# The first guess of 1/Q in MoE1's block 0: kept in the PSUM bank of h

## The chip, the cores and the metric

The kernel runs on one core of a Trainium2 chip. The metric is device time in microseconds (us) of one execution. Before the change the median of three runs is 865.55 us (864.24 to 868.3).

## The reference

Attention with two kinds of mask (local for heads 0 to 3, strided for 4 to 7) gives x, 2304 tokens by 512. A first MoE layer (MoE1) follows, which is a dense layer with a rational activation, and then a second (MoE2) that sends each token to the expert of its largest logit. Cut to what the change touches:

```python
def _moe_ref(x, w_in, w_out, a, b):        # x 2304x512, w_in 512x2048, w_out 2048x512
    h = x @ w_in
    h2 = h * h
    h3 = h2 * h
    P = a[0] + a[1] * h + a[2] * h2 + a[3] * h3
    Q = 1.0 + np.abs(b[0]) * np.abs(h) + np.abs(b[1]) * h2
    g = P / (Q + 1e-06)
    return (g @ w_out).astype(np.float32)
```

## The kernel before

MoE1 is cut into 6 blocks of 384 tokens, and each block into 16 slices of 128 hidden columns: 96 steps s, where block 0 is s = 0 to 15. Attention is cut into units U of one half of one pair of heads. While block 0 runs, units 8 to 15 still pass through, and the weights of MoE1 are still being split into high and low parts. All this is interleaved by hand, and each engine works off its own instructions in the order in which they are written.

One step passes through these named operations (the names are those of the order tables):

- `m1` (PE, line 516): 12 matmuls into a PSUM bank h. There are two such banks.
- `fA` (ACT, 446 and 447): A = |h| and G = a3 h + a2 in SBUF.
- `fP` (POOL, 451 and 452): Q = (b1 A + b0) A in SBUF, without the 1 of the reference.
- `fD`, `fE` (DVE, 457 and 462): G times h, then (G + a1) times h. `fE` is the last reader of h.
- `rA` (ACT, 470 and 472): Ln of Q + 1 + 1e-6, and Exp of its negative, which gives the first guess y of 1/Q. Either y takes the place of A in SBUF, or it goes into a PSUM bank m (steps 16 to 29, and 64 on).
- `rD`, `rN`, `rG` (DVE): one Newton step and the product with P. With y in A these are lines 481, 488 and 496, and both tensors of each come from SBUF. With y in PSUM they are 479, 486 and 493, and one of the two comes from PSUM.
- `sA` (ACT, 383) and `sP` (line 506, POOL or DVE): G into its high part gh and its low part gl. Then `m2` (PE, 527): 9 matmuls into three accumulators.

A unit of attention goes: `qk` (transposes of q and k on PE, copied out by DVE), `sc` (scores, 317), `mx` (row maxima, 340), `ex` (353), `rc` (363 and 365), `nm` (370, on POOL in this stretch), `aT` (transposes on PE, 379), `ae` (copy by ACT), `pv` (408), `xA` (ACT) and `xD` (DVE, 432). A weight is split by `c0A` (ACT, 223), `c0P` (POOL, 229), `c1` and `c1b` (DVE, 233 and 238), `c2A` (ACT or DVE, a cast on line 383) and `c2P` (249).

A window w covers the steps 2w and 2w+1. Its order is a table: `rD@-1` means "run rD up to step 2w-1 now, if what it needs has been written", and the letter after a point names the engine (A for ACT, D for DVE, G for POOL; with several letters they alternate). Windows 0 to 7, called "first", cover block 0. "plain" covers 8 to 14, "attention" 15 to 31, "last" 32 on. `ready` holds the conditions, among them free banks. A, Q and G have two buffers each, so `fA` of a step waits for `sP` two steps earlier.

Of the kernel before, what the change touches and what calls it, by code (L numbers as in the profile page):

```python
# [7 lines left out]
F32 = mybir.dt.float32  # L8
# [4 lines left out]
ACTF = mybir.ActivationFunctionType  # L13
ALU = mybir.AluOpType
# [5 lines left out]
def tile_attention_moe_moe2(  # L20
# [20 lines left out]
    BLK = 384  # L41
# [394 lines left out]
    hid = {}  # L436
# [193 lines left out]
    def keep_warm(n):  # L630
# [38 lines left out]
    def parse(text):
# [24 lines left out]
    done = {}  # L694
# [14 lines left out]
    def ready(T, j):  # L709
        for p, d in need[T]:  # L710
            if done[p] < j + 1 + d and not (j < 9 and (T, p) in (("mx", "aT"), ("ae", "pv"))):
                return False
        if T == "m1":
            i, f = divmod(j, NF)
            if i == 0 and done["c2P"] <= conv_q.index(("i", f)):
                return False
            if not all(log["h"][-1:]):
                return False
            if done["xD"] < (8, 16, 16, 24, 32, 32)[i]:
                return False  # L720
# [136 lines left out]
    def window(w, sch):  # L857
        if w == 8:
            load_w(len(conv_q) - n_load[0])
            for T, eng in (("c2A", "A"), ("c2P", "G"), ("c1b", ""), ("c1", ""), ("c0A", ""), ("c0P", "G")) * 4:  # L860
                run_to(T, len(conv_q), eng)
        if w == 32:
            for _ in range(3):
                run_to("rE", done["rT"], "A")
                run_to("rL", done["rT"], "")
                run_to("rP", done["rT"], "A")
                run_to("rQ", done["rT"], "")
        if w in (8, 15, 32):
# [506 lines left out]
```

## Time and profile before

| | |
|---|---|
| median of three runs | 865.55 us |
| the profiled execution: its own time, its span | 864.46 us, 862.7 us |
| mean granted TensorE clock, as a share of full speed | 0.970 |
| PE busy | 793.3 us, 92% |
| DVE busy | 688.3 us, 80% |
| ACT busy | 536.6 us, 62% |
| POOL busy | 464.1 us, 54% |

The span runs from the first to the last instruction. The engines' shares are means over stages: MoE1's block 0 lies at about 74 to 205 us, its other blocks up to about 620 us, MoE2 behind them. A wait that is told here is the idle time of an engine before an instruction, with what ended it.

### The profile page before, as it was taken

What the parts mean: (1) busy time and instruction counts of PE and PEld (TensorE: products, weight loads), DVE (VectorE), ACT (ScalarE), POOL (GpSimd) and SP (SyncE); (2) the same over time, 40 slices, a digit from 0 to 9 for tenths busy, and PEclk for the clock granted to TensorE, in tenths of its full rate; (3) what the DMA queues carried; (4) which work ended last, traced back from release to release, by engine and by line L of the source; (5) the groups of instructions that cost most, each with busy time, mean ns of one, the idle gap of its engine ahead of it and who ended that gap; (6) DMA issues with size and microseconds to landing.
All of it is one profiled execution on the core that took longest, in us unless ns stands there. A gap on an engine that the chain in (4) does not pass through costs nothing.

```text
span 862.7 us, 15597 instructions
## 1 busy us (share of the span) xinstructions
PE 793.3 (92%) x5301; PEld 678.0 (79%) x5301; DVE 688.3 (80%) x1656; ACT 536.6 (62%) x1397; POOL 464.1 (54%) x463
## 2 busy tenths in 40 slices
PE   6787687788999999999999999999899999999995
PEld 3555576677898787888878888888779999988884
DVE  4999989979777988789888889779865776777772
ACT  3786767565657787888776656666623554555552
POOL 3787878787554444443445668567423444444431
PEclk9989989889999999999999999999999999999998
DMA  8991322200201310122100100302115866776630
GB/s 198 307 263 49 104 84 68 57 8 12 63 1 28 82 45 12 42 61 69 44 9 8 38 2 2 134 1 100 62 27 185 319 220 229 226 240 226 225 117 5
DMA packets 71609, 85.59 MB, mean 99 GB/s; under 512 B 38111, under 2 KB 48607, under 8 KB 71520
## 3 DMA queue, kind: packets, MB, share of 16 engines
q1 hardware_dynamic: 68112, 74.36, 28.1%
q0 software_dynamic: 3120, 10.13, 3.6%
q8 instruction: 44, 0.72, 0.4%
q14 instruction: 45, 0.37, 0.1%
q10 hardware_dynamic: 288, 0.00, 0.0%
HBM read 74.89 MB, written 9.85 MB: 98 GB/s over the span
## 4 chain that ended last, share of the span: by engine, by line
PE 55%; DVE 19%; ACT 11%; POOL 7%; issue 4%; DMA 2%; SPq 0%; another core or an unknown queue 0%; POOLq 0%; DVEq 0%; ACTq 0%
PE h L516 13%; PE o L527 12%; PE h L1166 12%; PE o L1180 11%; ACT S L353 4%; DVE G L496 3%; DVE Q L488 2%; POOL Q L452 2%; DVE Q L481 2%; POOL Q L451 2%; ACT A L470 2%; POOL S L370 1%; ACT A L472 1%; PE m L379 1%; PE zb L632 1%
## 5 line engine op out<-in xcount | busy, mean ns | idle before, releaser
L516 PE MATMUL h<-xh,wi 128*128 128x384 f32 x768 | 219.2, 350 | 1.3 <-DVE G L462 1.3
L527 PE MATMUL o<-wo,gh 128*128 128x512 f32 x576 | 188.8, 409 | 2.1 <-POOL wo L249 1.8
L451 POOL TENSOR_SCALAR Q<-A,coef 128x384 f32<-128x384 f32 x96 | 80.3, 837 | 188.1 <-ACT A L446 187.8
L516 PEld LDWEIGHTS h<-xh,wi 128*128 128x128 f32 x768 | 145.2, 195 | 4.3 <-DVE G L462 2.0
L516 PE MATMUL h<-xl,wi 128*128 128x384 f32 x384 | 132.5, 345 | 4.7 <-DVE xl L432 4.7
L527 PEld LDWEIGHTS o<-wo,gh 128*128 128x128 f32 x576 | 105.8, 191 | 26.6 <-POOL wo L249 2.1
L527 PE MATMUL o<-wo,gl 128*128 128x512 f32 x288 | 116.3, 404 | 0.9 <-POOL gl L506 0.5
L452 POOL TENSOR_TENSOR Q<-Q,A 128x384 f32<-128x384 f32 x96 | 103.5, 1079 | 8.0
L1170 ACT ACTIVATE hh<-h 128x256 fp32r<-128x256 f32 x76 | 29.2, 384 | 98.5 <-PE h L1166 98.5
L1166 PE MATMUL h<-xh,w1h 128*128 128x256 f32 x320 | 89.5, 280 | 0.0
L1166 PE MATMUL h<-xh,w1l 128*128 128x256 f32 x320 | 89.0, 278 | 0.0
L1166 PE MATMUL h<-xl,w1h 128*128 128x256 f32 x320 | 88.9, 278 | 0.0
L470 ACT ACTIVATE A<-Q,coef 128x384 f32<-128x384 f32 x96 | 59.2, 616 | 45.2 <-POOL Q L452 45.0
L353 ACT ACTIVATE S<-S,nb 72x72 f32<-72x72 f32 (+1 forms) x224 | 80.6, 363 | 7.2 <-DVE nb L340 7.2
L516 PEld LDWEIGHTS h<-xl,wi 128*128 128x128 f32 x384 | 74.9, 195 | 6.6 <-DVE xl L432 5.0
L506 POOL TENSOR_TENSOR gl<-G,gh 128x384 fp32r<-128x384 f32 x71 | 74.7, 1052 | 9.6 <-ACT gh L383 9.4
L383 ACT CAST gh<-G 128x384 fp32r<-128x384 f32 x96 | 49.4, 514 | 42.0 <-DVE G L493 25.3
L446 ACT ACTIVATE A<-h 128x384 f32<-128x384 f32 x96 | 46.5, 485 | 40.6 <-PE h L516 40.4
L527 PEld LDWEIGHTS o<-wo,gl 128*128 128x128 f32 x288 | 55.0, 191 | 15.9 <-POOL gl L506 1.8
L457 DVE TENSOR_TENSOR G<-G,h 128x384 f32<-128x384 f32 x96 | 52.3, 545 | 17.1 <-ACT G L447 17.1
L447 ACT ACTIVATE G<-h,coef 128x384 f32<-128x384 f32 x96 | 63.9, 665 | 0.1
L1171 DVE SCALAR_TENSOR_TENSOR hl<-h,hh 128x256 fp32r<-128x256 f32 x76 | 32.2, 424 | 39.7 <-ACT hh L1170 39.7
(212 smaller groups left out, 1908.2 us busy)
## 6 DMA issues: line engine op xcount, KB each, us to landing
w1r<-in_moe_w_dram SPq DMA_DIRECT2D x36, 512.0 KB
w2r<-in_moe_w_dram SPq DMA_DIRECT2D x36, 512.0 KB
rawi<-in_moe_w_in_dram SPq DMA_DIRECT2D x16, 512.0 KB
rawo<-in_moe_w_out_dram SPq DMA_DIRECT2D x16, 512.0 KB
xs<-x SPq DMA_DIRECT2D x18, 256.0 KB
vt<-in_v_dram SPq DMA_DIRECT2D x48, 64.0 KB
rawq<-in_q_dram SPq DMA_DIRECT2D x16, 144.0 KB
rawk<-in_k_dram SPq DMA_DIRECT2D x16, 144.0 KB
```

The lines of the kernel that those rows point to most:

```text
L353: ACT.activation(out=Sv[:, j, c], in_=Sv[:, j, c], func=ACTF.Exp, scale=-1.0, bias=nb[0:nq, u : u + 1], **({"accum_out": rb[0:nq, u : u + ...
L383: (ACT.copy if eng is ACT else eng.tensor_copy)(out, in_)
L447: ACT.activation(out=G, in_=h, func=ACTF.Identity, scale=coef[:, 3:4], bias=coef[:, 2:3])
L451: eng.tensor_scalar(out=Q, in0=A, scalar1=coef[:, 5:6], scalar2=coef[:, 4:5], op0=ALU.mult, op1=ALU.add)
L452: eng.tensor_tensor(out=Q, in0=Q, in1=A, op=ALU.mult)
L457: DVE.tensor_tensor(out=G, in0=G, in1=h, op=ALU.mult)
L470: ACT.activation(out=A, in_=Q, func=ACTF.Ln, bias=coef[:, 6:7])
L506: eng.tensor_tensor(out=gl, in0=G, in1=gh.bitcast(F32), op=ALU.subtract)
L516: PE.matmul(h[:, 0:BLK], lhsT=w[:, o + 128 * kk : o + 128 * kk + 128], rhs=x[:, kk, c0 : c0 + BLK], start=n == 0, stop=n == 11)
L527: PE.matmul(acc[t], lhsT=a[:, ts], rhs=w[:, o : o + 512], start=f == 0 and n == 0, stop=f == NF - 1 and n == 2)
L1166: PE.matmul(h, lhsT=w[kk][:, 128 * f : 128 * f + 128], rhs=x[:, kk, c0 : c0 + TILE], start=n == 0, stop=n == 11)
L1180: PE.matmul(acc, lhsT=a[:, hs], rhs=w[f // 2][:, ws], start=f == 0 and n == 0, stop=f == NH - 1 and n == 2)
```

## The change

- For steps 0 to 14, `rA` writes y over h, in the same PSUM bank. The bank is free for `m1` two steps later only when `rG` has read y, where it was free after `fE` before. Step 15 uses a bank m like steps 16 to 29.
- `rD`, `rN` and `rG` of steps 0 to 15 take the forms with one tensor in PSUM.
- 1 + 1e-6 is written into the instructions (the bias of Ln, and a scalar of DVE), where it was read from a column of coef; the memset of that column goes.
- The order tables are new. In windows 1 to 7 the two steps of a window go side by side (`fD fD fE fE`, `rD rD rN rN rG rG`) rather than one after the other; `sP` of steps 0 to 14 is on DVE and no longer on POOL, and six of the seven casts `c2A` that DVE did are on ACT. On PE the two `m2` come ahead of the second `m1`, which now waits for `rG`, and `m2` runs one step later than before. In "plain" `sP` is all on POOL; in "attention" `pv` comes ahead of `sc`.

```diff
     def ew_p2(s):
         A, Q, G = st[s]
-        h = hid.pop(s)
+        h = hid[s] if y_home(s) == "h" else hid.pop(s)
         DVE.scalar_tensor_tensor(out=G, in0=G, scalar=coef[:, 1:2], in1=h, op0=ALU.add, op1=ALU.mult)
 
-    def y_in_psum(s):
-
-        return 16 <= s < 30 or s >= 64
+    def y_home(s):
+
+        return "h" if s < 15 else "m" if s < 30 or s >= 64 else "A"
 
     def ew_recip(s):
         A, Q, G = st[s]
-        ACT.activation(out=A, in_=Q, func=ACTF.Ln, bias=coef[:, 6:7])
-        y = misc("y")[:, 0:BLK] if y_in_psum(s) else A
+        ACT.activation(out=A, in_=Q, func=ACTF.Ln, bias=1.0 + 1e-6)
+        y = misc("y")[:, 0:BLK] if y_home(s) == "m" else hid.pop(s) if y_home(s) == "h" else A
...
     def ew_2(s):
         y, Q, G = st[s]
-        if y_in_psum(s):
-            DVE.scalar_tensor_tensor(out=y, in0=Q, scalar=coef[:, 6:7], in1=y, op0=ALU.add, op1=ALU.mult)
+        if y_home(s) != "A":
+            DVE.scalar_tensor_tensor(out=y, in0=Q, scalar=1.0 + 1e-6, in1=y, op0=ALU.add, op1=ALU.mult)
...
         "first": """
-        c1@-1 aT@-1 lw@-3 m1@0 c2P.D@-3 c1b@-1 ae.A@-1 fD@-1 pv@-1 c2A.AD@-3 sc@0 rA@-1 lq@0 fE@-1 fA@0
+        aT@-1 m1@0 c2P.D@-3 fD@-1 c1@-2 lq@0 c2A.AD@-3 ae.A@-1 pv@-1 fA@0 rD@0 lw@-3 c1b@-2 fP.G@0 c2A.A@-2 sc@0
...
             if not all(log["h"][-1:]):
                 return False
+            if j >= 2 and y_home(j - 2) == "h" and done["rG"] < j - 1:
+                return False
...
         elif T == "rD":
-            return not y_in_psum(j) or done["fE"] > j
-        elif T in ("pv", "rL", "rQ") or (T == "rA" and y_in_psum(j)):
+            return done["fE"] > j or y_home(j) == "A"
+        elif T in ("pv", "rL", "rQ") or (T == "rA" and y_home(j) == "m"):
             return can_alloc(1)
+        elif T == "rA":
+            return done["fE"] > j or y_home(j) == "A"
```

DVE at the end of window 5 and the start of window 6, before (the second step of the window from its `fE` on; S, rb and xl belong to attention, rawi and rawo are weights being split):

```order
L462 SCALAR_TENSOR_TENSOR G<-G,coef,h 128x384
L481 SCALAR_TENSOR_TENSOR Q<-Q,coef,A 128x384
L488 SCALAR_TENSOR_TENSOR Q<-Q,A 128x384
L496 SCALAR_TENSOR_TENSOR G<-G,coef,Q 128x384
L363 TENSOR_SCALAR rb<-rb 72x8
L365 RECIPROCAL rb<-rb 72x8
L432 TENSOR_TENSOR xl<-m,xh 128x288
L233 SCALAR_TENSOR_TENSOR rawi<-rawi 128x512
L233 SCALAR_TENSOR_TENSOR rawo<-rawo 128x512
L238 SCALAR_TENSOR_TENSOR rawi<-rawi 128x512
```

The same place after (line numbers are one lower there):

```order
L478 SCALAR_TENSOR_TENSOR G<-G,coef,h 128x384 x2
L485 SCALAR_TENSOR_TENSOR h<-Q,h 128x384 x2
L492 SCALAR_TENSOR_TENSOR G<-h,G 128x384 x2
L362 TENSOR_SCALAR rb<-rb 72x8
L364 RECIPROCAL rb<-rb 72x8
L431 TENSOR_TENSOR xl<-m,xh 128x288
L506 TENSOR_TENSOR gl<-G,gh 128x384 x2
L232 SCALAR_TENSOR_TENSOR rawi<-rawi 128x512
L232 SCALAR_TENSOR_TENSOR rawo<-rawo 128x512
L237 SCALAR_TENSOR_TENSOR rawi<-rawi 128x512
```

Both steps now pass through the three operations together, with h where A was, and two `sP` stand between `xD` and the splitting of the weights.

POOL in window 2, before:

```order
L229 TENSOR_SCALAR rawi<-rawi 128x512
L451 TENSOR_SCALAR Q<-A,coef 128x384
L452 TENSOR_TENSOR Q<-Q,A 128x384
L506 TENSOR_TENSOR gl<-G,gh 128x384
L229 TENSOR_SCALAR rawo<-rawo 128x512
L249 TENSOR_TENSOR wi<-rawi,wi 128x512
L249 TENSOR_TENSOR wo<-rawo,wo 128x512
L370 TENSOR_TENSOR S<-S,rb 72x576
L451 TENSOR_SCALAR Q<-A,coef 128x384
L452 TENSOR_TENSOR Q<-Q,A 128x384
L506 TENSOR_TENSOR gl<-G,gh 128x384
```

And after:

```order
L450 TENSOR_SCALAR Q<-A,coef 128x384
L451 TENSOR_TENSOR Q<-Q,A 128x384
L450 TENSOR_SCALAR Q<-A,coef 128x384
L451 TENSOR_TENSOR Q<-Q,A 128x384
L228 TENSOR_SCALAR rawi<-rawi 128x512
L228 TENSOR_SCALAR rawo<-rawo 128x512
L248 TENSOR_TENSOR wi<-rawi,wi 128x512
L248 TENSOR_TENSOR wo<-rawo,wo 128x512
L369 TENSOR_TENSOR S<-S,rb 72x576
```

Both `fP` have moved to the front, the two `sP` have gone, and `nm` (S<-S,rb) is the last of the window.

## Rows read from the trace of the kernel before

**Rows 1.** By stretch: length, busy PE, PEld, DVE, ACT, POOL, granted clock, DMA share, GB/s.

```profile
92.00:205.00 113.00, 91.45 (x569) 77.96 (x567) 101.96 (x220) 68.90 (x196) 90.98 (x77) 0.87 0.18 52
205.00:330.00 125.00, 121.49 (x793) 104.73 (x794) 101.73 (x249) 88.91 (x227) 58.37 (x61) 1.00 0.15 40
```

**Rows 2.** What PE waited for, 74 to 205 us: us in total, times, longest.

```profile
PE m L379 <- POOL S L370: 12.9, 5, 4.4
PE m L290 <- issue: 8.8, 3, 4.0
```

**Rows 3.** DVE by line and shape, 74 to 205 us: busy us, mean ns | idle before.

```profile
L496 DVE SCALAR_TENSOR_TENSOR G<-G,coef,Q 128x384 f32<-128x384 f32 x15 | 17.1, 1137 | 0.5
L488 DVE SCALAR_TENSOR_TENSOR Q<-Q,A 128x384 f32<-128x384 f32 x15 | 16.0, 1068 | 0.5
L481 DVE SCALAR_TENSOR_TENSOR Q<-Q,coef,A 128x384 f32<-128x384 f32 x15 | 13.6, 905 | 8.1 <-ACT A L472 7.0 <-POOL gl L506 1.0
...
L383 DVE COPY kT<-m 128x288 f32<-128x288 f32 x6 | 3.0, 536 | 0.1
...
L383 DVE CAST wi<-rawi 128x512 fp32r<-128x512 f32 x6 | 4.2, 694 | 0.0
```

**Rows 4.** DVE in window 2: start, us, instruction.

```profile
116.50 1.55 DVE L488 SCALAR_TENSOR_TENSOR Q<-Q,A 128x384 f32<-128x384 f32 x1
```

**Rows 5.** POOL in window 2.

```profile
116.14 1.49 POOL L249 TENSOR_TENSOR wi<-rawi,wi 128x512 fp32r<-128x512 f32 x1
...
120.11 1.15 POOL L370 TENSOR_TENSOR S<-S,rb 72x576 f32<-72x576 f32 x1 [0.90 <-ACT G L447]
```

**Rows 6.** DVE's forms with PSUM, whole span, by line.

```profile
L486 DVE SCALAR_TENSOR_TENSOR m<-Q,coef,m 128x384 f32<-128x384 f32 x46 | 28.3, 616 | 0.0
L479 DVE SCALAR_TENSOR_TENSOR G<-G,coef,m 128x384 f32<-128x384 f32 x46 | 28.1, 610 | 19.0 <-ACT m L472 19.0
L493 DVE SCALAR_TENSOR_TENSOR G<-m,G 128x384 f32<-128x384 f32 x46 | 25.6, 557 | 1.6
```

**Rows 7.** Line 506 on DVE: duration ns min/median/max, first and last start.

```profile
L506 DVE TENSOR_TENSOR gl<-G,gh x25: 549/567/1218, 210.8 to 619.9; 128x384 fp32r<-128x384 f32 x25
```

**Rows 8.** DVE at the end of window 1.

```profile
103.26 0.20 DVE L365 RECIPROCAL rb<-rb 72x8 f32<-72x8 f32 x1
...
103.70 0.68 DVE L233 SCALAR_TENSOR_TENSOR rawi<-rawi 128x512 uint32<-128x512 uint32 x1
```

**Rows 9.** POOL beside it.

```profile
103.63 3.57 POOL L370 TENSOR_TENSOR S<-S,rb 72x576 f32<-72x576 f32 x1 [0.90 <-DVE rb L365]
```

**Rows 10.** The chain that ended last: start, us, engine, tile, line.

```profile
107.25 0.69 PE m L379 x8
107.94 3.69 PE h L516 x12
...
158.99 2.34 PE h L516 x12
```

**Rows 11.** ACT by line and shape, 74 to 205 us.

```profile
L353 ACT ACTIVATE S<-S,nb 72x72 f32<-72x72 f32 x32 | 10.9, 341 | 0.0
L447 ACT ACTIVATE G<-h,coef 128x384 f32<-128x384 f32 x16 | 10.6, 661 | 0.0
L470 ACT ACTIVATE A<-Q,coef 128x384 f32<-128x384 f32 x15 | 9.3, 617 | 9.5 <-POOL Q L452 9.5
L472 ACT ACTIVATE A<-A 128x384 f32<-128x384 f32 x15 | 7.9, 525 | 0.5
...
L446 ACT ACTIVATE A<-h 128x384 f32<-128x384 f32 x16 | 7.6, 477 | 7.2 <-PE h L516 7.2
```

**Rows 12.** PE at the start of windows 1, 7 and 8.

```profile
90.58 0.82 PE L379 MATMUL m<-ident,S 96*128 96x96 f32 x6 [0.47 <-POOL S L370]
...
188.32 0.69 PE L379 MATMUL m<-ident,S 72*72 72x72 f32 x8 [1.30 <-POOL S L370]
...
201.99 0.52 PE L516 MATMUL h<-xh,wi 128*128 128x384 f32 x1
```

More of the change, by code (lines that the diff above doesn't have):

```diff
@@ L182, in tile_attention_moe_moe2 @@
                        fill=NEG, base=0, channel_multiplier=1)
-    coef = const.tile([128, 8], F32, name="coef")
+    coef = const.tile([128, 6], F32, name="coef")
     ACT.dma_start(out=coef[:, 0:4], in_=moe_a.rearrange("(o a) -> o a", o=1).to_broadcast([128, 4]))
@@ L189, in tile_attention_moe_moe2 @@
     DVE.scalar_tensor_tensor(out=coef[:, 4:6], in0=coef[:, 4:6], scalar=-1.0, in1=coef[:, 4:6], op0=ALU.mult, op1=ALU.max)
-    DVE.memset(coef[:, 6:7], 1.0 + 1e-6)
     wi = w_in.bitcast(U32).rearrange("(k p) w -> p k w", p=128)
@@ L477, in ew_1 @@
         y, Q, G = st[s]
-        if y_in_psum(s):
+        if y_home(s) != "A":
             DVE.scalar_tensor_tensor(out=G, in0=G, scalar=coef[:, 0:1], in1=y, op0=ALU.add, op1=ALU.mult)
         else:
-            DVE.scalar_tensor_tensor(out=Q, in0=Q, scalar=coef[:, 6:7], in1=y, op0=ALU.add, op1=ALU.mult)
+            DVE.scalar_tensor_tensor(out=Q, in0=Q, scalar=1.0 + 1e-6, in1=y, op0=ALU.add, op1=ALU.mult)
     def ew_2(s):
         y, Q, G = st[s]
-        if y_in_psum(s):
-            DVE.scalar_tensor_tensor(out=y, in0=Q, scalar=coef[:, 6:7], in1=y, op0=ALU.add, op1=ALU.mult)
+        if y_home(s) != "A":
+            DVE.scalar_tensor_tensor(out=y, in0=Q, scalar=1.0 + 1e-6, in1=y, op0=ALU.add, op1=ALU.mult)
         else:
@@ L491, in ew_3 @@
         y, Q, G = st[s]
-        if y_in_psum(s):
+        if y_home(s) != "A":
             DVE.scalar_tensor_tensor(out=G, in0=y, scalar=2.0, in1=G, op0=ALU.subtract, op1=ALU.mult)
-            release("y")
         else:
             DVE.scalar_tensor_tensor(out=G, in0=G, scalar=coef[:, 0:1], in1=Q, op0=ALU.add, op1=ALU.mult)
+        if y_home(s) == "m":
+            release("y")
     def ew_high(s, eng=ACT):
@@ L642, in tile_attention_moe_moe2 @@
         "start": """
-        kw@0 nm.GG@-2 kw@1 sc@0 pv@-3 c1b@-1 ln@0 ex.AA@-1 c0P.G@0 lw@0 rc@-1 c0A.A@0 aT@-2 mx@0 qk.D@1 c1@0
-        xA.A@-3 xD@-3 kw@2 ae.A@-2 c2A.AAA@-1 c2P.GG@-2
+        kw@0 nm.GG@-2 kw@1 sc@0 pv@-3 c1b@-1 ln@0 ex.AA@-1 c0P.G@0 lw@0 rc@-1 c0A.A@0 aT@-2 mx@0 qk.D@1 c1@0 xA.A@-3
+        xD@-3 kw@2 ae.A@-2 c2A.AAA@-1 c2P.GG@-2
         """,
         "first": """
-        c1@-1 aT@-1 lw@-3 m1@0 c2P.D@-3 c1b@-1 ae.A@-1 fD@-1 pv@-1 c2A.AD@-3 sc@0 rA@-1 lq@0 fE@-1 fA@0
-        c2A.A@-2 rD@-1 rN@-1 xA.A@-1 rG@-1 c0P.GG@-1 c1b@-2 fD@0 sA.A@-1 mx@0 fE@0 fP.G@0 rA@0 lw@0 c1@-2
@@ L649, in tile_attention_moe_moe2 @@
-        ex.A@0 rD@0 m2@-2 sP.DG@-1 c0A.AD@0 rN@0 rG@0 rc@0 c0P.G@0 xD@-1 c2P.G@-2 c0A.A@1 m1@1 nm.G@0 fA@1
-        qk.D@1 m2@-1 fP.GG@1 sA.A@0 sP.G@0
+        aT@-1 m1@0 c2P.D@-3 fD@-1 c1@-2 lq@0 c2A.AD@-3 ae.A@-1 pv@-1 fA@0 rD@0 lw@-3 c1b@-2 fP.G@0 c2A.A@-2 sc@0
+        rA@-2 fE@0 rN@0 lw@0 rG@0 fD@1 fE@0 xA.A@-1 c1b@-1 rA@0 c0P.GG@-1 sA.A@-1 mx@0 rD@1 ex.A@0 c1@-2 sP.DG@-1
+        rN@0 m2@-2 c0A.AD@-1 c0P.G@0 fA@1 m2@-2 rG@0 c0A.A@1 m1@1 rc@0 xD@-1 c2P.G@-2 sA.A@0 nm.G@0 qk.D@1 sP.D@0
+        fP.GG@1
@@ L651, in tile_attention_moe_moe2 @@
         """,
         "plain": """
-        m2@-3 rA@-1 m1@0 fA@0 xA.A@-2 sc@0 rD@-1 rN@-1 rG@-1 fP.G@0 ae.A@-1 lq@0 sA.A@-1 m1@1 mid@0 fD@0
-        fE@0 mx@0 rL@1 rP.A@1 rE.D@1 sP.D@-1 qk.A@1 rA@0 rT@0 m2@-2 rB@0 rD@0 rN@0 rG@0 mid@1 tail@1 aT@0
-        fA@1 fD@1 fE@1 sA.A@0 tail@0 rc@0 fP.G@1 end@1 xD@-1 nm.G@0 pv@0 sP.G@0 ex.A@0 end@0 rQ@1
+        xA.A@-2 rA@-1 m1@0 fA@0 rD@-1 m2@-3 rN@-1 rG@-1 lq@0 sc@0 fP.G@0 mid@0 m1@1 sA.A@-1 rL@1 rE.D@1 ae.A@-2 fD@0
+        rP.A@1 mx@0 qk.A@1 mid@1 fE@0 sP.GG@-1 rA@0 m2@-2 rD@0 end@0 rN@0 fA@1 fD@1 rB@0 tail@1 rT@0 rG@0 aT@0 rQ@1
@@ L656, in tile_attention_moe_moe2 @@
+        xD@0 ex.AA@0 fP.G@1 sA.A@0 end@1 fE@1 pv@0 rc@-1 sP.G@0 nm.D@0 tail@0
         """,
         "attention": """
-        m1@0 fP.G@-1 rA@-1 ae.A@-1 rD@-1 rN@-1 rG@-1 sc@0 pv@-1 fA@0 rB@0 mid@1 sA.A@-1 xA.A@-1 fP.G@0
-        tail@0 lq@0 mid@0 mx@0 m2@-2 sP.G@-1 rA@0 fD@0 fE@0 end@0 ex.A@0 rT@1 xD@-1 m1@1 rE.D@1 qk.A@1 end@1
-        rD@0 rN@0 rG@0 rc@0 fA@1 tail@1 nm.D@0 sA.A@0 m2@-1 fD@1 fE@1 rL@1 rP.A@1 sP.D@0 aT@0 rQ@1
+        m1@0 fP.G@-1 rA@-1 ae.A@-1 rD@-1 rN@-1 rG@0 pv@-1 fA@0 rB@0 mid@1 sc@0 sA.A@-1 xA.A@-1 fP.G@0 tail@0 lq@0
@@ L661, in tile_attention_moe_moe2 @@
+        mx@0 mid@0 m2@-2 end@0 sP.G@-1 fD@0 fE@0 xD@-1 rA@0 ex.A@0 rT@1 m1@1 rE.D@1 end@1 rD@0 rN@0 qk.A@1 rG@0 rc@0
+        fA@1 tail@1 nm.D@0 sA.A@0 m2@-1 fD@1 fE@1 rL@1 rP.A@1 sP.D@0 aT@0 rQ@1
         """,
         "last": """
-        y0@-1 end@1 nm.G@-1 rA@-1 pv@-1 m1@0 xA.D@-2 x0@0 mid@0 sP.G@-2 fA@0 rD@-1 rN@-1 rG@-1 sc@0 fP.G@0
-        aT@-1 rT@0 rE.A@1 m1@1 lq@0 x1@0 rB@0 fD@0 fE@0 xD@-1 y1@1 sA.A@-1 mid@1 sP.G@-1 tail@0 ae.D@-1 rA@0
-        end@0 mx@0 rD@0 rN@0 rG@0 rL@1 fA@1 fD@1 fE@1 ex@0 qk.A@0 m2@-2 fP.G@1 rP.A@1 rc@0 m2@-1 tail@1 rQ@1
@@ L666, in tile_attention_moe_moe2 @@
-        sA.A@0
+        m1@0 rA@-1 nm.G@0 pv@0 end@1 y0@-1 x0@0 xA.A@-2 sP.G@-2 rB@0 fA@0 rD@-1 aT@-1 rN@-1 sc@1 mid@0 rT@0 rG@-1
+        rE.A@1 fD@0 m1@1 x1@0 y1@1 fP.G@0 xD@-1 sA.A@0 fE@1 sP.G@-1 tail@0 rA@0 lq@0 rL@1 fA@1 rD@0 mid@0 end@0 rN@1
+        mx@0 fD@1 fP.G@1 rG@0 fE@1 qk.A@0 m2@-2 ae.D@-2 ex@0 rP.A@1 rc@0 m2@-1 tail@1 sA.A@0 rQ@1
         """,
@@ L868, in window @@
         if w in (8, 15, 32):
-            for T, eng in (("m1", ""), ("fA", ""), ("fP", "G"), ("fD", ""), ("fE", ""), ("m2", "")):
-                run_to(T, 2 * w - 2 * (T == "m2"), eng)
+            for T, eng in (("m1", ""), ("fA", ""), ("fP", "G"), ("fD", ""), ("fE", ""), ("rA", ""), ("rD", ""), ("rN", ""), ("rG", ""),
+                           ("sA", "A"), ("sP", "G")) * 2 + (("m2", ""),):
+                run_to(T, 2 * w - (1 if T[0] == "r" or T == "sA" else 2 if T in ("sP", "m2") else 0), eng)
         e = even.get(2 * w + 4, 0)
@@ L1251, in tile_attention_moe_moe2 @@
     for _ in range(9):
-        if done["m2"] < NS:
+        if done["m2"] < NS or not done["y1"]:
             window(NS // 2 + 1, PLAN["last"])
```

## The prediction

> **What bounds the kernel now.** I read the stretches first [rows 1]. From 205 us on PE works nearly without a gap (121.5 of 125 us) at the full granted clock, so nothing is to be had there by relieving another engine. In block 0 it is otherwise: from 92 to 205 us PE is busy for 91.5 of 113 us, at a mean granted clock of 0.87, that is, partly at the lower of its two levels (1.2 and 2.4 GHz). DVE is busy for 102.0 and POOL for 91.0. A shorter block 0 shifts all that follows, since PE goes straight on.
>
> Second, PE's waits in this stretch [rows 2]: 12.9 us for `nm` on POOL in five places, and 8.8 us at `qk`, where the profile names no releaser (four transposes go through three banks that DVE empties). So the weights' and the attention's work on POOL and DVE releases PE.
>
> Third, why DVE is so busy. The three operations `rD`, `rN`, `rG` take 905, 1068 and 1137 ns on average [rows 3]; the forms with one tensor in PSUM do as much arithmetic in 610, 616 and 557 [rows 6]. One of the long ones took 1.55 us exactly while POOL ran a subtraction of 1.49 us that had begun just before [rows 4, 5]. In reverse, `nm` took 3.57 us on POOL where DVE began a weight shift 0.07 us behind it and that shift kept its 0.68 [rows 8, 9]; undisturbed the same shape takes 1.15 [rows 5]. So here an operation of DVE with two SBUF tensors and one of POOL wait for each other, whole instructions at a time.
>
> The Trainium skill says the same (SBUF — State Buffer, section "Who interferes with whom"): a DVE instruction with two SBUF inputs and a GpSimd one that reads SBUF exclude each other for the whole instruction, and one with at most one SBUF input does not contend. By that rule the three operations leave the contest, but `sP`, now on DVE with two SBUF inputs, enters it; this is weighed again under the slower rival.
>
> **The change part by part.**
>
> *y over h.* 15 steps times (905+1068+1137−610−616−557) ns = 15 x 1.33 = 19.9 us less on DVE [rows 3, 6]. y in a bank h is not in this trace; the nearest rows are those with a bank m, and the tensors differ in nothing else, so I take these.
>
> *`sP` from POOL to DVE.* 15 instructions of between 549 and 1218 ns [rows 7]: 8.2 to 18.3 us more. I take 0.6 each, 9 us, since they mostly stand beside a POOL that has less to do. *Casts.* Six of DVE's casts go to ACT: 6 x 0.69 = 4.2 us less [rows 3]. *Step 15* loses another 1.3 us. DVE's sum is −19.9 −1.3 −4.2 +9 = −16 us, with −7 at the long end of `sP`. POOL loses 15 `sP`.
>
> *What takes over.* DVE had about 16 us per window (six windows from 90.58 to 188.32 us are 97.7 us, 16.3 each [rows 12]) and would now need about 14. But a new ring closes: a bank h is free only after `rG`, all of both steps goes in pairs, and `nm` stands last. From the end of `nm` to the end of the next one:
> - `aT` on PE 0.69, then the even `m1` 2.34 to 3.69, by PE's clock [rows 10]: 3.0 to 4.4.
> - its `fA` on ACT 0.48+0.66 [rows 11]: 4.2 to 5.5. The odd step's `m1` was run before `aT` and its `fA` lies beside.
> - on ACT two casts and `xA`, at the 0.69 of DVE's cast [rows 3] about 2.0: 6.2 to 7.5. `fP` on POOL lies beside these.
> - two `rA`, 2 x (0.62+0.53) [rows 11]: 8.5 to 9.8. DVE's `c1`, `c1b`, `fD`, `fE` and `mx` lie beside.
> - `ex`, 8 x 0.341 [rows 11]: 11.2 to 12.5. `rD` to `rG` of both steps, six operations of 0.6, lie beside and end at much the same time.
> - `rc`, of which the last instruction is 0.20, and 0.17 until `nm` starts [rows 8, 9]; with the first instruction 0.5: 11.7 to 13.0. `nm` 1.15 [rows 5]: 12.9 to 14.2.
>
> I take the middle, 13.5, for windows 1, 3, 5 and 6. Windows 2 and 4 have a `qk`, whose four copies of 0.54 [rows 3] PE waits for ahead of the next `aT`: 2.1 to 2.9 more, I take 16. Six windows: 4 x 13.5 + 2 x 16 = 86, so −11.7 us against 97.7.
>
> *The end of block 0.* From `aT` of window 7 to the first `m1` of window 8 it is 201.99−188.32 = 13.7 us before [rows 12]. Now `m1` of step 15 waits for `rG` of step 13, about 10.5 into the ring, then takes 2.3 to 3.7, and the `m2` that runs a step later than before comes next with about as much: 15 to 18. I take 15.5, 2 us later.
>
> *The rest.* The immediates: Ln with a bias from SBUF takes 617 ns, Exp without one 525 [rows 11]; 0 to 0.09 us per step, which in the ring is within its bounds, and later lies beside PE's matmuls: nothing. "plain", "attention" and "last" move work between engines that PE does not wait for while it is at 121.5 of 125 us; if that cover went, a window there would show it on PE, and I leave 2 us either way. Window 0 keeps its order on the path (its `m1` are not gated by `rG`): nothing.
>
> Sum: −11.7 +2 = about −10. The profiled execution took 864.46 us, 1.8 more than its span and 1.1 below the median of the runs; 864.46−10 = 854.5. I say **854**.
>
> **The rivals.**
>
> 1. *The ring runs at its short end.* With PE at the upper clock throughout, ACT's instructions overlapping a little and the two `qk` hidden under `sP`, a window is 12.9 and one with `qk` 14: 4 x 12.9 + 2 x 14 = 79.6, −18, window 7 unchanged: **846**. For it: DVE's sum of −16. Against it: PE still stands idle before `rG` in each window, and idle PE came back at half the clock (3.69 against 2.34 [rows 10]).
>
> 2. *Mostly given back.* The ring at its long end, 4 x 14.2 + 2 x 17.1 = 91, is −6.7, and window 7 costs 4: **862**. For it: the same half clock, now for the odd `m1` too. Against it: gaps of PE become shorter than the up to 4.4 us of before [rows 2].
>
> 3. *Slower: `sP` shuts `nm` out.* `sP`, and the weight shifts behind it, stand just behind `xD`, where `nm` wants to begin. If DVE gets in first, as in window 1, `nm` takes 3.57 in place of 1.15 [rows 5, 9], 2.4 us in each of the six windows. On my mean window of 86/6 = 14.3 that gives 16.7; on the long one of 15.2, 17.6. Against 16.3 it is slower from a delay of 2.0 per window on: 6 x 0.4 + 2 = +4 to 6 x 1.3 + 4 = +12, so 868 to 876, say **871**. Against it: `sP` needs `sA`, and `sA` stands behind `ex` and two scalings on ACT; three instructions at the 0.69 of a cast [rows 3] are 2.1 us, while `nm` can begin 0.5 behind `ex`. By the rule of the Trainium skill named above, whoever starts first keeps the ports for its whole instruction, so it would hang on that order alone.
>
> 4. *No effect.* Block 0 becomes shorter, but what follows waits for something else, transfers above all, and the time is lost again: **864**. Against it: no long wait of PE after 205 us [rows 1].
>
> **How the numbers follow.** Forecast 0.55 (its own range 848 to 860), rival 1 0.17, rival 2 0.13, rival 3 0.09, rival 4 0.06. A difference below 0.5%, which is 861.2 to 869.9 us, can't be told from none here. Faster than that: 0.55+0.17 and 0.08 of rival 2, 0.80. Within: 0.05 of rival 2, 0.06 of rival 4 and 0.02 of rival 3, 0.13. Slower: 0.07. The range of 845 to 863 holds the forecast, rival 1 and most of rival 2.
>
> **What would show it.** Right: from the `aT` of window 1 to that of window 7 about 86 us in place of 97.7; no `rD`, `rN`, `rG` there above 0.7 us; PE's wait before the odd `m1`, ended by DVE's `rG`; saturation of PE about 10 us earlier. Wrong: `nm` of 2.5 us or more in most windows (rival 3); even `m1` at 3.7 in every window with `nm` short (rival 2); new gaps of PE behind 205 us (rival 4, or a fault in the tables for the later windows, which I have costed at nothing).

## The result and the profile after

The changed kernel takes **841.83 us** (median of four runs, 841.75 to 845.17); the kernel before, run beside it, 865.04 (864.24 to 868.3). The ratio is **0.973, with a 95% interval of 0.970 to 0.977**. The profiled execution took 841.75 us with a span of 840.0 at a mean granted clock of 0.980, against 864.46, 862.7 and 0.970 before. The forecast of 854 was too slow by 12 us, and the time lies below the range of 845 to 863.

Where the 22.7 us of the span went, by the starts of PE's instructions in the two traces:

| stretch | before, us | after, us | difference |
|---|---|---|---|
| `aT` of window 1 to `aT` of window 7 ("the six windows") | 97.7 | 78.4 | −19.3 |
| on to the first `m1` of window 8 | 13.7 | 14.0 | +0.3 |
| on to `m1` of step 30 | 65.0 | 62.9 | −2.0 |
| on to `m1` of step 63 | 197.9 | 195.9 | −2.0 |
| the rest, before window 1 and behind step 63 | | | +0.3 |

The two stretches of the trace after, with the columns of [rows 1]:

```profile
92.00:205.00 113.00, 100.22 (x667) 85.19 (x666) 94.36 (x257) 85.22 (x233) 81.22 (x79) 0.98 0.22 66
205.00:330.00 125.00, 121.96 (x842) 104.34 (x841) 97.92 (x278) 89.59 (x254) 58.73 (x62) 1.00 0.14 35
```

Against [rows 1] PE executes 98 more instructions in the first stretch, at 0.98 of the full clock in place of 0.87, and the second stretch is as full as it was. What PE waited for from 74 to 205 us, as in [rows 2] (`qk` is on line 289 here):

```profile
PE h L516 <- DVE G L492: 11.0, 7, 2.8
PE h L516 <- DVE xl L431: 4.7, 1, 4.7
PE m L378 <- POOL S L369: 3.5, 5, 2.1
PE m L289 <- PE m L289: 0.7, 1, 0.7
...
PE m L289 <- DVE qT L382: 0.3, 1, 0.3
```

The wait for `nm` has shrunk from 12.9 to 3.5 us, and the wait at `qk` from 8.8 to 1.0. The new wait, for a bank h that `rG` frees, is there as foretold, but it is at most 2.8 us long, in window 1, where the `m1` behind it took 3.92 us. All later `m1` of block 0 took 2.33 to 2.36. DVE and POOL by line, 74 to 205 us:

```profile
L506 DVE TENSOR_TENSOR gl<-G,gh 128x384 fp32r<-128x384 f32 x15 | 9.1, 645 | 1.6 <-ACT gh L382 1.6
L478 DVE SCALAR_TENSOR_TENSOR G<-G,coef,h 128x384 f32<-128x384 f32 x15 | 9.1, 610 | 3.0 <-ACT h L471 2.9
L485 DVE SCALAR_TENSOR_TENSOR h<-Q,h 128x384 f32<-128x384 f32 x15 | 7.7, 554 | 0.0
L492 DVE SCALAR_TENSOR_TENSOR G<-h,G 128x384 f32<-128x384 f32 x15 | 7.7, 549 | 0.0
...
L369 POOL TENSOR_TENSOR S<-S,rb 72x576 f32<-72x576 f32 x4 | 4.6, 1149 | 3.0 <-ACT rawo L222 2.6 <-DVE rb L364 0.4
L369 POOL TENSOR_TENSOR S<-S,rb 96x768 f32<-96x768 f32 x3 | 4.4, 1467 | 2.4 <-ACT rawo L222 1.5 <-ACT rawi L222 0.8
```

The three operations take 610, 554 and 549 ns in place of 905, 1068 and 1137 [rows 3], and no `nm` is held back any more (1149 and 1467 are also the shortest of their shapes). Last, window 6 of the changed kernel, PE and then ACT: start, duration, instruction, and in brackets the idle time before it:

```profile
157.03 0.69 PE L378 MATMUL m<-ident,S 72*72 72x72 f32 x8 [0.22 <-POOL S L369]
157.52 0.42 PE L516 MATMUL h<-xh,wi 128*128 128x384 f32 x1
...
161.16 0.73 PE L527 MATMUL o<-wo,gh 128*128 128x512 f32 x2
...
165.22 0.40 PE L527 MATMUL o<-wo,gl 128*128 128x512 f32 x1
166.68 0.45 PE L516 MATMUL h<-xh,wi 128*128 128x384 f32 x1 [1.06 <-DVE G L492]
...
169.25 0.44 PE L378 MATMUL m<-ident,S 72*72 72x72 f32 x4 [0.21 <-POOL S L369]
...
161.95 0.76 ACT L382 CAST xh<-m 128x288 fp32r<-128x288 f32 x1
162.45 0.59 ACT L469 ACTIVATE A<-Q 128x384 f32<-128x384 f32 x1
163.06 0.50 ACT L471 ACTIVATE h<-A 128x384 f32<-128x384 f32 x1
163.53 0.53 ACT L469 ACTIVATE A<-Q 128x384 f32<-128x384 f32 x1
164.09 0.50 ACT L471 ACTIVATE h<-A 128x384 f32<-128x384 f32 x1
164.52 0.34 ACT L352 ACTIVATE S<-S,nb 72x72 f32<-72x72 f32 x1
```

From one `aT` to the next PE stands still for 1.3 us by the brackets. The two `m2`, 161.16 to 165.62, lie just where PE would wait for the bank h. On ACT the next instruction mostly begins before the duration of the one ahead is over (162.45 against 161.95 + 0.76).

### The profile page after: what moved, and what is told of

Its sections match the earlier page's. It is cut to its first block, busy times and chain, and to the rows that moved or that the text cites. A ratio compares the mean times of both kernels' runs of the same rounds, so it can differ in the third digit from the quotient of the medians.

```text
span 840.0 us, 15609 instructions
## 1 busy us (share of the span) xinstructions
PE 784.4 (93%) x5294; PEld 670.0 (80%) x5301; DVE 649.1 (77%) x1657; ACT 531.0 (63%) x1403; POOL 442.8 (53%) x455
## 4 chain that ended last, share of the span: by engine, by line
PE 61%; DVE 16%; ACT 9%; POOL 5%; issue 3%; DMA 3%; SPq 2%; another core or an unknown queue 0%; POOLq 0%; DVEq 0%; ACTq 0%
PE h L516 16%; PE o L527 15%; PE h L1170 12%; PE o L1184 12%; ACT S L352 4%; POOL Q L451 2%; POOL Q L450 2%; DMA rawk<-in_k_dram 1%; ACT A L469 1%; PE m L378 1%; DMA rawi<-in_moe_w_in_dram 1%; DVE rawo L232 1%; PE m L1143 1%; DVE S L369 1%; DVE S L339 1%
## 5 line engine op out<-in xcount | busy, mean ns | idle before, releaser
L527 PE MATMUL o<-wo,gh 128*128 128x512 f32 x576 | 185.2, 403 | 0.0
L450 POOL TENSOR_SCALAR Q<-A,coef 128x384 f32<-128x384 f32 x96 | 76.2, 794 | 183.9 <-ACT A L445 183.8
L516 PEld LDWEIGHTS h<-xh,wi 128*128 128x128 f32 x768 | 142.6, 191 | 17.2 <-DVE G L492 14.0
L527 PE MATMUL o<-wo,gl 128*128 128x512 f32 x288 | 114.0, 396 | 0.0
L469 ACT ACTIVATE A<-Q 128x384 f32<-128x384 f32 x96 | 50.7, 528 | 35.2 <-POOL Q L451 34.9
L506 POOL TENSOR_TENSOR gl<-G,gh 128x384 fp32r<-128x384 f32 x63 | 64.7, 1027 | 11.7 <-ACT gh L382 11.1
L527 PEld LDWEIGHTS o<-wo,gl 128*128 128x128 f32 x288 | 54.1, 188 | 13.5 <-POOL gl L506 0.4
```

The source lines that it names most:

```text
L450: eng.tensor_scalar(out=Q, in0=A, scalar1=coef[:, 5:6], scalar2=coef[:, 4:5], op0=ALU.mult, op1=ALU.add)
L469: ACT.activation(out=A, in_=Q, func=ACTF.Ln, bias=1.0 + 1e-6)
L506: eng.tensor_tensor(out=gl, in0=G, in1=gh.bitcast(F32), op=ALU.subtract)
L516: PE.matmul(h[:, 0:BLK], lhsT=w[:, o + 128 * kk : o + 128 * kk + 128], rhs=x[:, kk, c0 : c0 + BLK], start=n == 0, stop=n == 11)
L527: PE.matmul(acc[t], lhsT=a[:, ts], rhs=w[:, o : o + 512], start=f == 0 and n == 0, stop=f == NF - 1 and n == 2)
```

## The experiments

Each ratio is against the kernel before, run beside it on the same chip; "the six windows" are 97.7 us before and 78.4 after, and each kernel's are read from its one profiled execution. The runs came from several chips, on which the kernel before took 865.0 to 869.3 us. The first question was which of the parts brings it: y in PSUM, the order, `sP` on DVE, or the clock that goes with them.

### The order without y in PSUM

```
-        return "h" if s < 15 else "m" if s < 30 or s >= 64 else "A"
+        return "A" if s < 15 else "m" if s < 30 or s >= 64 else "A"
```

The conditions of the order still treat the steps 0 to 14 as if y were in h, so every engine has the order of the changed kernel; the immediates are in, too.

> The changed kernel, but y of steps 0 to 14 is in A in SBUF again (rD, rN, rG read two tensors of SBUF); every engine's order is that of the changed kernel, m1 included. Theory A (the ports that DVE and POOL share are what block 0 was short of, and y in PSUM frees them): the three operations go back to about 1 us each, DVE gains 15 x 1.2 = 18 us, and most of the gain is lost: 855 to 860 us. Theory B (the new order, by pairs and with sP on DVE, brings the gain): 842 to 848. Theory C (PE's clock stays up because the new order leaves PE shorter gaps): 842 to 848, with a granted clock of 0.95 or more from 92 to 180 us.

Measured: 866.81 us, ratio 0.997 (0.995 to 0.999); six windows 97.0 us. The order alone brings nearly nothing, less than even theory A left it (855 to 860). Its window 1, POOL and then DVE:

```profile
100.98 4.08 POOL L248 TENSOR_TENSOR wi<-rawi,wi 128x512 fp32r<-128x512 f32 x1
105.02 1.28 POOL L248 TENSOR_TENSOR wo<-rawo,wo 128x512 fp32r<-128x512 f32 x1
106.27 1.46 POOL L369 TENSOR_TENSOR S<-S,rb 72x576 f32<-72x576 f32 x1
...
100.87 1.02 DVE L484 SCALAR_TENSOR_TENSOR Q<-Q,A 128x384 f32<-128x384 f32 x2
101.81 1.02 DVE L491 SCALAR_TENSOR_TENSOR Q<-Q,A 128x384 f32<-128x384 f32 x2
102.75 1.14 DVE L498 SCALAR_TENSOR_TENSOR G<-G,coef,Q 128x384 f32<-128x384 f32 x2
```

With two SBUF tensors each, the six operations that the new order puts in a row keep their 0.5 to 0.6 us, and `c2P` on POOL takes 4.08 in place of about 1.3. `nm` stands behind it, and PE behind `nm`: PE's waits for `nm` are 21.2 us from 74 to 205 us, the longest 7.5. With y in h the same `c2P` of window 1 begins beside the same six operations, and takes 1.29 in the changed kernel:

```profile
97.88 1.29 POOL L248 TENSOR_TENSOR wi<-rawi,wi 128x512 fp32r<-128x512 f32 x1
```

### y in PSUM without the order

The kernel before, its tables, with y of steps 0 to 14 over h; `rA` had to move behind `fE`:

```
-        ... pv@-1 c2A.AD@-3 sc@0 rA@-1 lq@0 fE@-1 fA@0
+        ... pv@-1 c2A.AD@-3 sc@0 lq@0 fE@-1 rA@-1 fA@0
```

> The kernel before, in its old order on every engine, but y of steps 0 to 14 in the bank of h. Theory A: DVE loses 15 x 1.3 = 20 us and POOL's waits become shorter, so 846 to 851. Theory B: 860 to 865. Theory C: between, 855 to 862, since the gaps of PE before aT are those of nm, which stands where it stood.

Measured: 860.65 us, ratio 0.992 (0.989 to 0.994); six windows 90.6 us. So the parts don't add up: −0.8% and −0.3% alone, −2.7% together.

### `sP` on either engine, in either order

Three kernels, each with an `sP` moved: the changed one with `sP` of block 0 on POOL, the one with the old order and y in h with `sP` on DVE, and the one with the new order and y in SBUF with `sP` on POOL.

```
-  ... sP.DG@-1 ... sP.D@0          (changed kernel)
+  ... sP.G@-1 ... sP.G@0
-  ... sP.DG@-1 ... sP.G@0          (old order, y in h)
+  ... sP.D@-1 ... sP.D@0
-  ... sP.DG@-1 ... sP.D@0          (new order, y in SBUF)
+  ... sP.G@-1 ... sP.G@0
```

> The changed kernel with sP of steps 0 to 14 on POOL instead of DVE, at the same place behind nm. Theory A: DVE is relieved by 15 x 0.66 = 10 us, but POOL has two sP of 1.0 ahead of the next window's fP; A and G come free later, and the ring that goes through fP becomes longer by up to 2 us per window: 845 to 855. If DVE's time were still the bound of block 0 (the rival to the ring): faster, 834 to 840.

> The old order with y in h, and sP of steps 0 to 14 on DVE at its old places. Theory D (formed on the first four runs: what counts is how long two-input operations of DVE and operations of POOL stand against each other; y in h alone moves the contention to the weight shifts, which took 1.0 to 1.2 us, and sP off POOL takes it away): the shifts fall towards 0.7 us and the six windows from 90.6 us to 85 or less: 850 to 855. Rival E (the pairing of the steps is what is missing): no better than with sP on POOL, 858 to 863.

> The new order with y in SBUF and sP on POOL: the last corner of the cube of y, order and sP. By theory D the pairs in SBUF contend with the weights' subtraction on POOL all the more, as POOL has two more operations: 868 to 876. If the order alone were good once DVE has no sP: 855 to 862.

Measured, the first: 847.98 us, 0.974 (0.971 to 0.978), six windows 84.4. Its profile is of the slowest of four runs (852.49 us, the fastest took 843.08). The second: 863.08 us, 0.996 (0.995 to 0.997), 93.9. The third: 862.68 us, 0.995 (0.993 to 0.997), 96.5, where theory D had 868 to 876. So the old order isn't cured by taking `sP` off POOL, which refutes the theory that only the sum of the mutual waits of DVE and POOL counts: what their instructions took over the shortest of the same line and shape fell from 23.0 to 16.1 us in the six windows, and the windows went from 90.6 to 93.9. In the new order `sP` on POOL costs little over the whole, but brings back what the rival 3 spoke of, in the windows 1 and 5 (POOL's `nm`):

```profile
101.83 3.57 POOL L369 TENSOR_TENSOR S<-S,rb 72x576 f32<-72x576 f32 x1 [0.43 <-ACT rawo L222]
...
158.64 3.57 POOL L369 TENSOR_TENSOR S<-S,rb 72x576 f32<-72x576 f32 x1 [0.43 <-DVE rb L364]
```

### The clock alone

The kernel before, with 24, 12, 24 and 6 matmuls of 128x128, into the bank that `aT` writes next, ahead of `aT` of the units 10, 12, 14 and 15 (windows 2, 4, 6 and 7), so that PE does not stand idle while it waits:

```
+        for _ in range(WARM.get(U, 0)):
+            PE.matmul(banks[0][:, 0:128], lhsT=ident, rhs=ident, start=True, stop=True)
```

> The kernel before, with 24, 12, 24 and 6 extra matmuls of 128x128 (into the bank that aT writes next) ahead of aT of units 10, 12, 14 and 15, so that PE is not idle while it waits for nm. Theory C (clock is the main cause): granted clock above 0.93 from 92 to 180 us and 848 to 855 us. Theories A and B: the even m1 takes 2.1 to 2.4 in place of 3.7 in up to four windows, which is at most 4 x 1.5 = 6 us, and part of that waits for DVE anyway: 859 to 864.

Measured: 868.85 us, ratio 1.001 (0.999 to 1.003); six windows 95.8. The stretch from 92 to 180 us, columns as in [rows 1], in the kernel before and then in this one:

```profile
92.00:180.00 88.00, 70.12 (x452) 60.40 (x452) 78.61 (x178) 54.50 (x157) 69.37 (x59) 0.85 0.22 65
92.00:180.00 88.00, 79.47 (x596) 70.69 (x595) 81.07 (x180) 56.81 (x162) 72.53 (x62) 0.92 0.22 68
```

The granted clock in this stretch rose from 0.85 to 0.92, the even `m1` of the windows 2, 4 and 6 came down from 3.88, 3.89 and 4.19 us to 2.33, and yet the whole did not become faster, where even the theories A and B had 859 to 864. So in the old order PE's clock is not what block 0 was short of. Whether the higher clock of the changed kernel (0.98 there) adds to its gain, no run shows.

### What in the new order counts: PE's place for `m2`

Two kernels with a difference on PE alone: the old order and y in h, with the transposes of `qk` behind the odd step's `m2`; and the changed kernel with the odd `m1` ahead of the two `m2`.

```
-  m1@1 nm.G@0 fA@1 qk.D@1 m2@-1 fP.GG@1       (old order, y in h)
+  m1@1 nm.G@0 fA@1 m2@-1 qk.D@1 fP.GG@1
-  rN@0 m2@-2 ... fA@1 m2@-2 rG@0 c0A.A@1 m1@1 rc@0        (changed kernel)
+  rN@0 ... fA@1 rG@0 c0A.A@1 m1@1 m2@-2 m2@-2 rc@0
```

> The kernel with the order of before and y of steps 0 to 14 over h, with one change: on PE the four transposes of qk come behind the odd step's m2 and no longer ahead of it; every other engine's order is the same. Theory E (part of what the old order costs is PE standing in line before qk, 8.2 us in three places, with m2 and the next aT and m1 behind it): the windows 2 and 4 (16.0 and 18.4 us) come down by 2 to 3 us each, aT of window 1 to aT of window 7 takes 85 to 87 us instead of 90.6, the whole 855 to 857 us, ratio 0.985 to 0.988. Rival F (the old order is dear for the sequence on DVE and POOL, where nm stands behind the weights' work; PE only shows it): windows 2 and 4 within 1 us of theirs, 90 us, 860 us, ratio 0.991.

> The changed kernel with one difference: on PE the odd step's m1 comes ahead of the two m2, as it does before the change; the other engines' order is the same. Theory E (what PE has to do while a bank h is not yet free decides): m1 waits for rG with the two m2 behind it, which then run between m1 and the next aT. Nine matmuls of m2 are about 1.9 us each, so each of the windows gets 1 to 2 us longer: aT of window 1 to aT of window 7 84 to 90 us instead of 78.4, the whole 848 to 853 us, ratio 0.979 to 0.984. Rival F (the order on DVE and POOL is what brings the gain): m2 finds room behind m1 since aT waits for nm anyway; 78 to 80 us, 842 to 843 us, ratio 0.972 to 0.974.

Measured, the first: 859.56 us, ratio 0.993 (0.990 to 0.995), six windows 92.8. The windows 2 and 4 came down from 16.0 and 18.4 to 15.2 and 14.9, but 3 and 5 went up to 15.5 and 18.5. PE's wait at `qk` became one for the bank h:

```profile
PE m L379 <- POOL S L370: 11.6, 5, 3.9
PE h L521 <- DVE G L497: 6.5, 3, 3.0
PE m L290 <- issue: 2.2, 1, 2.2
```

The place of `qk` isn't what the old order costs: theory E is wrong there, and so is F in part, which had the windows 2 and 4 within 1 us of theirs. The second: **880.91 us, ratio 1.018 (1.015 to 1.021)**, six windows 109.0, so two groups of matmuls in another place cost 39 us, where theory E had 6 to 11 and theory F none. What it waited for the bank h in block 0 (11.0 in the changed kernel), and PE in its window 4:

```profile
PE h L516 <- DVE G L492: 40.4, 7, 6.4
...
148.13 0.90 PE L316 MATMUL m<-kT,qT 64*96 64x128 f32 x12
154.63 0.69 PE L516 MATMUL h<-xh,wi 128*128 128x384 f32 x1 [5.59 <-DVE G L492]
...
158.21 0.63 PE L527 MATMUL o<-wo,gh 128*128 128x512 f32 x2
...
162.17 0.39 PE L527 MATMUL o<-wo,gl 128*128 128x512 f32 x1
162.41 0.67 PE L289 MATMUL m<-ident,rawq 72*128 72x72 f32 x8
162.91 0.93 PE L289 MATMUL m<-ident,rawk 72*128 72x72 f32 x8
163.83 0.57 PE L378 MATMUL m<-ident,S 96*128 96x96 f32 x4
```

PE waits 5.59 us for the bank with nothing to do, `m1` then takes 3.75 (154.63 to 158.38) where it takes 2.3 after an unbroken stretch, and the two `m2` of 4.2 stand ahead of the next `aT`. In the changed kernel they fill the wait. y over h makes this wait; only with the `m2` in it is it harmless.

### What in the new order counts: `sP` ahead of the shifts

The changed kernel with a difference on DVE alone: in block 0 the two `sP` behind the first two weight shifts.

```
-  aT@-1 m1@0 c2P.D@-3 fD@-1 c1@-2 lq@0 ... nm.G@0 qk.D@1 sP.D@0
+  aT@-1 m1@0 c2P.D@-3 fD@-1 c1@-2 sP.D@-1 lq@0 ... nm.G@0 qk.D@1
```

> The changed kernel with one difference, on DVE alone: in the windows of block 0 the two sP stand behind the first two weight shifts (232) and no longer ahead of them, so that nothing holds DVE back from a shift when xD ends, about 0.5 us after nm has begun on POOL. Theory of the prediction's slower rival (an operation of DVE with two SBUF tensors that stands right behind xD shuts nm out): nm takes 2.5 to 3.6 us instead of 1.15 to 1.47 in most of the windows 1 to 7, six windows 84 to 92 us instead of 78.4, the whole 848 to 856 us, ratio 0.979 to 0.989. Theory of the ring (nm has begun and the shift waits for it): nm stays at 1.15 to 1.5, a shift takes some 1.5 us, which lies beside PE's work, six windows 78 to 80 us, 842 to 844 us, ratio 0.972 to 0.975.

Measured: 853.78 us, ratio 0.982 (0.980 to 0.983); six windows 86.7. Against the 0.973 of the changed kernel that is some 7 us, and 8.3 in the six windows. It is inside what was expected from rival 3, though `nm` was held in two windows, 1 and 5, not in most. These two are 5.3 of the 8.3 us; the windows 2 and 6, where `nm` kept its 1.15, are 3.0 longer, and why was not traced. Its window 5, POOL and then DVE:

```profile
158.91 4.50 POOL L369 TENSOR_TENSOR S<-S,rb 72x576 f32<-72x576 f32 x1 [0.84 <-DVE rb L364]
...
158.98 0.68 DVE L232 SCALAR_TENSOR_TENSOR rawi<-rawi 128x512 uint32<-128x512 uint32 x1
159.58 0.69 DVE L232 SCALAR_TENSOR_TENSOR rawo<-rawo 128x512 uint32<-128x512 uint32 x1
160.18 1.02 DVE L506 TENSOR_TENSOR gl<-G,gh 128x384 fp32r<-128x384 f32 x2
161.12 0.68 DVE L237 SCALAR_TENSOR_TENSOR rawi<-rawi 128x512 uint32<-128x512 uint32 x1
161.72 0.68 DVE L237 SCALAR_TENSOR_TENSOR rawo<-rawo 128x512 uint32<-128x512 uint32 x1
```

`nm` shows as begun 0.07 us ahead of the first shift, and yet all six DVE operations run at their undisturbed durations and `nm` ends only behind the last of them. In its window 6 the order is the other way:

```profile
175.87 1.15 POOL L369 TENSOR_TENSOR S<-S,rb 72x576 f32<-72x576 f32 x1 [1.45 <-ACT rawo L222]
...
176.27 1.90 DVE L232 SCALAR_TENSOR_TENSOR rawo<-rawo 128x512 uint32<-128x512 uint32 x2
```

Here the shift comes 0.40 us behind, `nm` keeps its 1.15, and the two shifts take 1.90 in place of 1.28. In the changed kernel `sP` stands between and waits for `sA` on ACT, so that DVE's next operation with two SBUF tensors begins 0.81 us behind `nm` (168.86 and 168.05 us in window 6), and `nm` keeps its 1.15.

### The later tables and the immediates

The changed kernel with the tables "plain", "attention" and "last" of before; the changed kernel with 1 + 1e-6 read from coef again; and the kernel before with the immediates alone:

```
-        ACT.activation(out=A, in_=Q, func=ACTF.Ln, bias=coef[:, 6:7])
+        ACT.activation(out=A, in_=Q, func=ACTF.Ln, bias=1.0 + 1e-6)
```

(and the same in the two DVE operations; the second kernel has it the other way round).

> The changed kernel with the order of before in windows 8 on (the tables plain, attention and last). Block 0 as in the changed kernel (78.4 us from aT of unit 9 to that of unit 15). If the 2.0 us that were gained between steps 16 and 32 and the 2.0 us between 32 and 64 come from the new later tables, 844.5 to 847; if they are left over from block 0 (PE's warm clock, what was buffered when it ended), 841 to 843.

> The changed kernel with 1 + 1e-6 read from a column of coef again, by Ln and by DVE. Ln takes 617 ns in place of 535, rN 616 in place of 550; both lie in the ring of block 0, twice and up to four times per window: 7 x (0.16 to 0.3), so 1 to 2 us slower, and nothing later; the rival (they lie beside other work) says 0.

> The kernel before with 1 + 1e-6 written into Ln and into DVE's two operations, and nothing else changed; the order on every engine is that of before. Theory I (about 1.3 to 2 us of the gain behind block 0 come from these immediates, since m1 of step 30 to that of step 63 took 195.9 to 196.0 us in each kernel with them and 197.2 to 197.9 in each without): this stretch goes from 197.9 to 196, and a little more elsewhere, ratio 0.996 to 0.999. Rival (that stretch is faster for something else that those kernels share, such as the later tables): 197.9, ratio 0.999 to 1.001.

Measured: 842.38 us, ratio 0.972 (0.970 to 0.974), so the later tables bring nothing that can be told from none. Without the immediates 844.25 us, 0.974 (0.971 to 0.977): in the medians that is 1.9 above the kernel just named, on the same chip, which the intervals don't tell apart. Its six windows are 77.4 us, so the loss that was expected in block 0 isn't there. The immediates alone: 864.27 us, **ratio 0.994 (0.993 to 0.996)**, a gain of 5.0 us in the medians where 1 to 3.5 were expected. ACT and DVE from 205 to 600 us in that kernel:

```profile
L470 ACT ACTIVATE A<-Q 128x384 f32<-128x384 f32 x77 | 40.6, 528 | 34.4 <-POOL Q L452 34.1
...
L486 DVE SCALAR_TENSOR_TENSOR m<-Q,m 128x384 f32<-128x384 f32 x43 | 23.9, 555 | 0.0
L481 DVE SCALAR_TENSOR_TENSOR Q<-Q,A 128x384 f32<-128x384 f32 x35 | 19.6, 561 | 11.3 <-ACT A L472 11.2
```

Ln is 0.09 us shorter than with the bias from SBUF (617 in [rows 11]), DVE's operation 0.06 (616 in [rows 6]). From `m1` of step 30 to that of step 63 it is 196.1 us, as in the changed kernel (195.9), against 197.9 before. These 2 us are the immediates, as theory I had it: the stretch is 195.9 to 196.1 us in all eight kernels that have them, and 197.2 to 197.9 in the six that read the constant from SBUF. The other 3 us of the gain are not located: the trace of this kernel and that of the kernel before, which did not run side by side, differ by 0.6 us in the whole span. The new order with y in SBUF has the immediates too, and at 0.997 it is no faster than they are alone. So nothing shows that the order by itself brings anything.

## Why the prediction was wrong

- **What bounds the kernel**: right in the main. Block 0 gave 19.0 of the 22.7 us, and PE's stretch behind 205 us stayed full. But "nothing is to be had there" was off by some 2 us, those of the immediates.
- **y over h**: right. 15 x (610+554+549) is 21.0 us less than the 15 x 3110 ns of before; 19.9 were put down, and most of the difference is the immediate in `rN` (554 in place of 616 ns). `sP` on DVE measured 9.1 us where 9 was taken. DVE's busy time from `aT` of window 0 to the first `m1` of window 8 fell from 117.2 to 96.4 us, 20.9 where 16 was summed.
- **The ring**: the links were right and the sum was too long; this is the step that failed. Window 6 after, from the end of one `nm` at 156.97 us: `m1` ends 2.9 later (3.0 to 4.4 given), `xA` gives way to `rA` at 5.5 (6.2 to 7.5), `rA` ends at 7.6 (8.5 to 9.8), `ex` at 10.4 (11.2 to 12.5), `nm` at 12.2 (12.9 to 14.2). I added up whole durations, and successive instructions of ACT start before the duration of the one ahead is over; and I took the middle of PE's two clocks, though a PE with the `m2` in its gap had the upper one. "I take the middle, 13.5": windows 1, 3, 5 and 6 took 13.1, 13.6, 12.6 and 12.2, in all 2.4 us less.
- **The windows with `qk`**, "I take 16": 13.6 and 13.3, in all 5.2 us less. About half of this is the ring again: from `aT` to the end of `nm` it took 12.0 and 12.5 us here. The other half is `qk`. Its transposes begin before `nm` ends, so they delay the next `aT` only by what is left behind it: that starts 1.6 and 0.8 us behind the end of `nm`, where 2.1 to 2.9 were put down (it is 0.05 in the windows 3, 5 and 6, and 1.7 in window 1, behind the `m1` of 3.92). The ring's own miss is thus about 4.9 us, the largest of all.
- **The end of block 0**, +2: it was +0.3. `m1` of step 15 starts 9.7 us behind `aT` of window 7, where 10.5 was given, and it and the `m2` behind it begin 2.2 and 2.1 ahead of what follows them, at the short end of the 2.3 to 3.7 put down for each.
- **The rest**, "nothing": about −3.7. Some 2 of it are the immediates, shown; 2 more lie ahead of step 30, from a cause that stays open. For the immediates PE's busy time misled me: PE was busy for 121.5 of 125 us from 205 to 330 us, and yet the 0.15 us per step that ACT and DVE saved showed at PE, some 0.055 of it in each of the steps 30 to 62.
- **Rival 1** had the mechanism and the sizes of the six windows: 4 x 12.9 + 2 x 14 = 79.6, measured 51.6 + 26.8 = 78.4. Its 846 is still 4 us too slow, for the rest, which it had at nothing too. It got 0.17 because I took idle PE before `rG` to mean half the clock. That is so (the kernel with `m1` ahead of `m2` shows a granted clock of 0.83 from 92 to 180 us, and 3.75 us for an `m1` behind 5.59 us of waiting), but the idle time was filled.
- **Rival 3** did not occur, for the reason given against it: `sP` waits for `sA`. The mechanism is real. With two DVE operations in another place the kernel loses some 7 us, of which 5.3 in the windows where `nm` was held. The rule of the Trainium skill (SBUF — State Buffer, section "SBUF: two separate sides"), that whoever comes first keeps the ports for its whole instruction, agrees with the lead of 0.40 us above; with a lead of 0.07 by the profile the measurement says that DVE has them (in 15 of 16 cases), and keeps them over six instructions in a row.
- **Rivals 2 and 4**: the even `m1` of window 6 takes 2.3 us (157.52 to 159.86), not 3.7, and the 19 us were not lost behind block 0.

What stays open: why the old order with y in h still needs 15 to 18 us in most windows. `qk` ahead of `m2`, and `sP` on POOL, are excluded as the single cause; one `nm` there is held (3.57 us in window 1), but the rest was not taken apart. Of the new order, the pairing of the steps and the casts moved to ACT were not tried by themselves.

## What to carry to other kernels

When a buffer is freed later than before, put work into the queue of the waiting engine ahead of the instruction that will wait: here, in the changed kernel, that place alone decided between a ratio of 0.973 and one of 1.018. Read a change of data placement and the order that goes with it as one thing, since neither had more than a third of the gain alone. In a chain of short instructions add the spacings of starts, not the durations, and try a constant operand as an immediate: here that alone brought 0.6%.

## What the runs showed of the hardware

- A run of DVE operations with two SBUF tensors can hold a POOL instruction out to the end of the run: 4.50 us for `nm` behind six, 3.57 behind four shifts [rows 8, 9 show the first], 1.15 undisturbed. Where `nm` came first, the two engines could also take turns: the four shifts behind the `nm` of window 3, in the old order with y in h, took 1.95, 0.99, 1.49 and 1.49 us.
- In all fourteen kernels, an `nm` whose start is recorded 0.07 to 0.08 us ahead of a DVE operation with two SBUF tensors was held in 15 of 16 cases; with a lead of 0.28 us or more it was never held by that operation (23 cases).
- A constant from SBUF costs Ln 0.09 us (617 against 528 ns) and DVE's operation 0.06 us (616 against 555) on 128x384.
